# Attention with a noisy top-2 router on one core: another order around the last attention tile, and one-hots of two groups on ScalarE

## The chip, the cores and the metric

The kernel runs on one core of a Trainium2 chip. A core has five engines with an instruction queue each: TensorE (PE: matmuls and transposes; its weight loads are listed apart as PEld), VectorE (DVE), ScalarE (ACT), GpSimd (POOL) and SyncE (SP, which here only issues DMAs). Each works through its queue in order and waits on semaphores for the others; transfers are done by 16 DMA engines that all queues share. The metric is the device time of one execution in microseconds; the time before is the median of three runs.

## The reference

Chunked attention with a few memory rows, then a mixture of experts in which each row goes to its two best experts. Cut to what matters:

```python
# attention: B 4, H 8, S 768, D 64; chunks of 32 rows, context 16 left, 8 right, 8 memory rows
scores = scale * q_c @ concat(mem_k, k_ctx).T
a = exp(scores - scores.max(-1));  a = a / (a.sum(-1) + 1e-9)
out = a @ concat(mem_v, v_ctx)
# router: x (3072, 512), 8 experts
noisy = x @ w_gate + log1p(exp(x @ w_noise)) * noise
top2 = the two largest of noisy per row;  top2_w = softmax over these two
# experts
for e in range(8): out[rows with e] += top2_w * (relu(x[rows] @ w1[e]) @ w2[e])
```

## The kernel before

**Attention.** The 3072 rows are cut into 12 tiles of 256 rows. A loop of slots (-1 to 11) runs a software pipeline: slot i makes the scores of tile i+1 and the values of tile i, and turns the x rows of tile i-1 (in the last slot also those of tile 11) for the router's gate. The order inside a slot is written out by hand, as one string of letters per slot (ORDERS), and the queues of TensorE, ScalarE, VectorE and SP follow that order. GpSimd has its own queue: pinned instructions keep the order in which the program calls them, and its work on the routing is put among them as it is called.

The letters that matter here: S scores, s their maximum and subtraction (settle_s, L530 and L532), E the exponential (L603), W the transposes of a window of values (p_v, L490), w and y their copy to SBUF. The copy of the second window also issues, on SP, two DMAs that bring the memory rows of values next to it (mvn, L500) and two that store finished x rows to DRAM (xd, L679). P is the transpose of the probabilities (p_p, L610), p its copy (pT, L616), V the row sums and values (ps_g L623, ps_o L630; ps_o reads the window and the memory rows), i the reciprocal, v and v1 the two norms (L643), X, X2 and X3 transposes of x rows, x, x2 and x3 their copies to xT, G the gate (ps_l, L665), g and r its copy to lg on VectorE or ScalarE.

**Routing.** A Route handles a group of tiles: R[0] tiles 0 to 6, R[1] tiles 7 to 9, R[2] tiles 10 and 11. Since a tile has two halves of 128 rows, they have 14, 6 and 4 half tiles. N starts a route and makes its noise on ScalarE (two ACTIVATEs, L293 and L294). C steps through `choose` on VectorE, 14 instructions that find the two best experts and code the pair (the matrix M, in ohp). K ranks the rows of each pair on TensorE (`ranks`, p_rank) and adds up the counts on GpSimd (`total`, cum; the next group's ranks need it). H turns p_rank into one rank per row. O (`slots`) makes a one-hot of 96 places per row, `weights` and `values` the numbers that are to be listed (row, row of the output, three parts of a weight, a flag), on GpSimd for R[0] and R[1]. Q and q multiply one-hots with the first two values on TensorE: the list of rows (`list_rows`, L384). F does the same with the other four (`list_facts`, L389). Letter a adds the lists of rows and makes main_src, the indices of the first gather. Rows past the 96 places of a pair go to a rest list: I (`rest_onehots`) makes one-hots of 64 rest places, T (`rest_list`, L403) multiplies them.

**Experts.** After slot 11 the rows are gathered by index from xd (L978, GpSimd), 96 for each pair of experts; the first eight tiles are turned on TensorE (p_xt, L1204), later ones by transposing DMAs. Then the eight experts follow one another (p_h L1032, p_y L1096), with weights in five rotating places. `load_layer(2, 0)` is the first load of expert 2, 1 MB, issued on GpSimd behind slot 9:

```python
    WHEN = {9: [(2, 0)]}
```

It stands in GpSimd's queue ahead of the weights of R[1].

Of the kernel before, what the change touches and what calls it, by code (L numbers as in the profile page):

```python
# [16 lines left out]
Alu = mybir.AluOpType  # L17
# [6 lines left out]
def kernel(  # L24
# [14 lines left out]
    nc = tc.nc  # L39
# [237 lines left out]
    class Route:  # L277
# [64 lines left out]
        def weights(self, eng):  # L342
            d = self.tile([128, self.n], F32, "d")
            eng.tensor_tensor(out=d, in0=self.mm[:, 1], in1=self.mm[:, 0], op=Alu.subtract)
            for i in range(3):
                eng.tensor_copy(self.f[:, :, 2 + i], d)
                if i < 2:
                    eng.tensor_tensor(out=d, in0=d, in1=self.f[:, :, 2 + i], op=Alu.subtract)
            self.eng.tensor_tensor(out=self.f[:, :, 5], in0=self.ii[:, 0], in1=self.ii[:, 1], op=Alu.is_gt)
# [17 lines left out]
        def slots(self):  # L367
            n, eng = self.n, self.eng
            self.oh_l = (self.tile([128, n, MT], BF16, "oh_l") if self.last else
                         nat[2 * self.k].rearrange("p g c -> p (g c)")[:, 0:n * MT].rearrange("p (n t) -> p n t", n=n))  # L370
            eng.tensor_tensor(out=self.oh_l, in0=bc(self.rr, MT), in1=io_l[:, 0:MT].unsqueeze(1).to_broadcast([128, n, MT]), op=Alu.is_equal)
# [20 lines left out]
    def rest_onehots(r):  # L392
        t1 = const.tile([128, r.n], F32, name=f"t1{r.k}")
        nc.vector.tensor_scalar(out=t1, in0=r.rr, scalar1=float(MT), scalar2=None, op0=Alu.is_ge)
        k2 = const.tile([128, r.n], F32, name=f"k2{r.k}")
        nc.vector.scalar_tensor_tensor(out=k2, in0=r.rr, scalar=1.0 - MT, in1=t1, op0=Alu.add, op1=Alu.mult)
        nc.vector.tensor_tensor(out=oh_t[:, r.g0:r.g0 + r.n], in0=bc(k2, RU),
                                in1=io_1[:, 0:RU].unsqueeze(1).to_broadcast([128, r.n, RU]), op=Alu.is_equal)
# [293 lines left out]
    def decode(L, n, name, src=None, pool=const):  # L692
# [27 lines left out]
    WHEN = {9: [(2, 0)]}  # L720
# [14 lines left out]
    ]  # L735

    with tc.manual_schedule(engines={ET.PE, ET.Activation, ET.DVE, ET.SP}):
# [11 lines left out]
        def close(r):  # L749
            advance(r.chain)  # L750
            if r.last:
                r.values(nc.gpsimd, 0, 2)
            else:
                r.weights(nc.gpsimd)
                r.values(nc.gpsimd, 0, NV)

        def weigh(r):
            r.weights(nc.vector)
            r.values(nc.vector, 2, NV)
# [10 lines left out]
        def slot(i):  # L770
# [124 lines left out]
            for g, x in enumerate("AB"):  # L895
# [5 lines left out]
                      Q=lambda r: (r.list_rows(p1[:, 0], r is R[-2], r is R[-1]), r.list_facts(p2, r is R[-2], r is R[-1])),  # L901
                      q=lambda r: r.list_rows(p1[:, 0], r is R[-2], r is R[-1]),
                      F=lambda r: r.list_facts(p2, r is R[-2], r is R[-1]))
            for k in ORDERS[i + 1].split():
# [6 lines left out]
                elif k == "Y":  # L911
                    pin(nc.gpsimd.indirect_dma_start(out=turning[3].bitcast(F32)[0:MT, 0:E], out_offset=None, in_=moe_w_gate,
                                                     in_offset=bass.IndirectOffsetOnAxis(ap=ready[0:MT], axis=0)))
                elif k[0] == "I":
                    rest_onehots(R[int(k[1])])
# [5 lines left out]
                elif k == "a":  # L921
                    nc.vector.tensor_tensor(out=src[0:MT], in0=p1[:, 0], in1=listed[0:MT, 0], op=Alu.add)
                elif k[0] in rs and k not in fs:
                    rs[k[0]](R[len(RG) - 1 if k.endswith("2") else -1 if i < NT - 1 else len(RG) - 2])
                else:
                    fs[k]()
# [5 lines left out]
            for e, n in WHEN.get(i, ()):  # L932
                load_layer(e, n)
# [624 lines left out]
```

## Time and profile before

| | |
|---|---|
| Median of three runs | 334.56 us (334.29, 334.56, 336.42) |
| Profiled execution, its own time | 333.11 us |
| Its span, first to last instruction | 331.5 us |
| Mean granted TensorE clock | 0.926 |
| TensorE busy | 278.4 us (84%) |
| VectorE, ScalarE, GpSimd busy | 185.7 (56%), 153.5 (46%), 209.0 us (63%) |
| TensorE busy from 105 to 130 us | 3.25, 2.95, 3.87, 3.38, 4.51 of every 5 us |
| TensorE busy from 130 to 150 us | 10.00 and 9.95 of every 10 us |

How to read it: a busy share is an average over the program. Up to about 104 us the attention keeps four engines busy side by side; from about 135 us on TensorE does the experts with hardly a pause. Between these lies the routing of the last tiles, where every engine waits for another. Rows of a timeline give the start, the length, the engine, the line, what is written and read, how many instructions were merged, and in brackets how long the engine had stood idle before and what released it.

### The profile page before, as it was taken

What the parts mean: (1) busy time and instruction counts of PE and PEld (TensorE: products, weight loads), DVE (VectorE), ACT (ScalarE), POOL (GpSimd) and SP (SyncE); (2) the same over time, 40 slices, a digit from 0 to 9 for tenths busy, and PEclk for the clock granted to TensorE, in tenths of its full rate; (3) what the DMA queues carried; (4) which work ended last, traced back from release to release, by engine and by line L of the source; (5) the groups of instructions that cost most, each with busy time, mean ns of one, the idle gap of its engine ahead of it and who ended that gap; (6) DMA issues with size and microseconds to landing.
All of it is one profiled execution on the core that took longest, in us unless ns stands there. A gap on an engine that the chain in (4) does not pass through costs nothing.

```text
span 331.5 us, 9214 instructions
## 1 busy us (share of the span) xinstructions
PE 278.4 (84%) x3746; PEld 206.3 (62%) x3762; DVE 185.7 (56%) x418; ACT 153.5 (46%) x316; POOL 209.0 (63%) x304
## 2 busy tenths in 40 slices
PE   0566979888799578999999999999999999999920
PEld 0455867777677368866766775585676666767400
DVE  4765755979798885644653443835345345443520
ACT  5666644766676202535453453453543534525210
POOL 4679595999482457767768675743754744735370
PEclk9969797999979755999999999999999999999975
DMA  7999959988926513435587895998979789522141
GB/s 126 212 211 192 216 109 219 219 138 119 225 51 117 132 30 80 97 79 111 86 182 123 87 182 120 191 217 143 224 151 215 171 158 186 130 83 74 58 145 37
DMA packets 43501, 46.79 MB, mean 141 GB/s; under 512 B 20465, under 2 KB 33845, under 8 KB 43452
## 3 DMA queue, kind: packets, MB, share of 16 engines
q0 software_dynamic: 23024, 38.27, 60.3%
q1 hardware_dynamic: 19884, 7.83, 11.7%
q8 instruction: 31, 0.51, 0.6%
q14 instruction: 18, 0.15, 0.1%
q10 hardware_dynamic: 544, 0.03, 0.1%
HBM read 59.11 MB, written 11.33 MB: 212 GB/s over the span
## 4 chain that ended last, share of the span: by engine, by line
PE 59%; DMA 6%; DVE 6%; issue 3%; ACT 2%; POOL 1%; POOLq 0%; SPq 0%; DVEq 0%; ACTq 0%
PE p_h L1032 28%; PE p_y L1096 21%; DMA w_all<-mvn 5%; PE p_y L1151 2%; PE p_v L490 1%; POOL out_dram L983 1%; PE ps_o L630 1%; ACT pT L616 1%; PE p_t L461 1%; DMA xt<-xd,main_src 1%; ACT w_all L465 1%; PE p_xt L1204 1%; PE p_p L610 0%; PE p_x L652 0%; PE p_rank L338 0%
## 5 line engine op out<-in xcount | busy, mean ns | idle before, releaser
L1032 PE MATMUL p_h<-w_all 128*128 128x288 bf16 (+3 forms) x1120 | 97.5, 248 | 0.7 <-ACT w_all L465 0.5
L1032 PEld LDWEIGHTS <-w_all 128*128 128x128 bf16 x1120 | 83.6, 99 | 14.0 <-issue 2.1
L1096 PE MATMUL p_y<-w_all 128*128 128x512 bf16 x368 | 83.6, 379 | 2.1 <-DVE yq L1090 0.8
L1020 ACT ACTIVATE w_all<-p_h 128x288 bf16<-128x288 f32 (+3 forms) x137 | 46.8, 375 | 45.4 <-PE p_h L1032 42.3
L1096 PEld LDWEIGHTS <-w_all 128*128 128x128 bf16 x384 | 37.1, 98 | 43.6 <-issue 2.1
L437 POOL COPY w_all<-w_all 128x512 bf16<-128x512 bf16 (+1 forms) x59 | 42.9, 795 | 12.2 <-PE p_t L461 7.4
L1018 DVE TENSOR_SCALAR w_all<-p_h 128x288 bf16<-128x288 f32 (+1 forms) x65 | 30.7, 476 | 34.2 <-PE p_h L1032 34.0
L983 POOL DMA_INDIRECT out_dram<-y,main_dst x24 | 22.8, 949 | 18.6 <-DMA w_all<-in_moe_w_dram 5.8
L1105 DVE SCALAR_TENSOR_TENSOR y<-p_y,main_w,y 96x512 f32<-96x512 f32 x24 | 17.9, 747 | 26.0 <-PE p_y L1096 26.0
L978 POOL DMA_INDIRECT xt<-xd,main_src x28 | 26.0, 928 | 10.0 <-issue 7.0
L1090 ACT COPY yr<-p_y 32x512 f32<-32x512 f32 x24 | 13.9, 579 | 36.4 <-DVE y L1105 34.6
L1101 ACT ACTIVATE y<-p_y,main_w 96x512 f32<-96x512 f32 x24 | 16.4, 683 | 21.5 <-PE p_y L1096 21.5
L461 PE MATMUL p_t<-identf,w_all 128*128 128x128 f32 x120 | 19.0, 297 | 1.8 <-ACT pT L616 0.8
L1000 POOL DMA_INDIRECT out_dram<-yB,rd x8 | 9.3, 1160 | 16.8 <-DVE yB L1157 15.6
L1090 DVE COPY yr<-p_y 32x512 f32<-32x512 f32 x12 | 8.3, 694 | 19.8 <-ACT y L1101 19.8
L1262 POOL DMA_INDIRECT fr<-tdr,adr x16 | 16.0, 1000 | 4.9 <-issue 4.6
L978 POOL DMA_INDIRECT xt<-xd,rs x16 | 14.8, 925 | 6.7 <-issue 3.4
L490 PE MATMUL p_v<-identf,w_all 128*128 128x128 f32 x96 | 16.4, 312 | 2.8 <-ACT w_all L465 1.8
L643 DVE TENSOR_TENSOR w_all<-ps_o,rs 128x512 bf16<-128x512 f32 x24 | 15.7, 683 | 5.0 <-PE ps_o L630 4.2
L461 PEld LDWEIGHTS p_t<-identf,w_all 128*128 128x128 f32 x120 | 14.3, 152 | 3.5 <-issue 1.6
L465 ACT COPY w_all<-p_v 128x512 f32<-128x512 f32 x21 | 12.0, 587 | 9.1 <-PE p_v L490 9.0
L1090 DVE COPY yq<-p_y 32x512 f32<-32x512 f32 x12 | 8.3, 694 | 12.9 <-ACT y L1101 12.8
(237 smaller groups left out, 419.6 us busy)
## 6 DMA issues: line engine op xcount, KB each, us to landing
w_all<-in_moe_w_dram POOLq DMA_DIRECT2D x12, 1024.0 KB
w_all<-in_moe_w_dram POOLq DMA_DIRECT2D x16, 256.0 KB
w_all<-in_k_dram POOLq DMA_DIRECT2D x4, 768.0 KB
w_all<-in_q_dram POOLq DMA_DIRECT2D x4, 768.0 KB
w_all<-in_v_dram POOLq DMA_DIRECT2D x4, 768.0 KB
xd<-w_all SPq DMA_DIRECT2D x24, 128.0 KB
w_all<-mvn SPq DMA_DIRECT2D x24, 32.0 KB
w_all<-xt SPq DMA_TRANSPOSE x39
```

The lines of the kernel that those rows point to most:

```text
L437: i = eng.tensor_copy(to, x)
L461: nc.tensor.transpose(out=p_t[:, s, :], in_=m.bitcast(F32)[:, s * 128:(s + 1) * 128], identity=identf)
L490: nc.tensor.transpose(out=p_v[:, i, c, :], in_=vT[:, c, c0:c0 + 128], identity=identf)
L978: pin(nc.gpsimd.indirect_dma_start(out=t[0:n].bitcast(I32), out_offset=None, in_=src_, in_offset=bass.IndirectOffsetOnAxis(ap=ix, axis=0)))
L983: i = nc.gpsimd.indirect_dma_start(out=out if rows is None else rows, out_offset=bass.IndirectOffsetOnAxis(ap=ix, axis=0), in_=y, in_offse ...
L1018: nc.vector.tensor_scalar(out=out_, in0=in_, scalar1=0.0, scalar2=None, op0=Alu.max)
L1020: nc.scalar.activation(out=out_, in_=in_, func=Act.Relu)
L1032: nc.tensor.matmul(out=o if len(xk.shape) == 2 else o.rearrange("p (j t) -> p j t", j=xk.shape[1]), lhsT=w_all[:, e % WR, kp * F + f * 128 ...
L1090: (nc.scalar.copy if eng else nc.vector.tensor_copy)(to, p[MT:128, :])
L1096: nc.tensor.matmul(out=p, lhsT=h[:, f, k, :], rhs=w2(e, f), start=(f == 0), stop=(f == FB - 1))
L1101: nc.scalar.activation(out=y[0:MT], in_=p[0:MT], func=Act.Copy, scale=wt)
L1105: nc.vector.scalar_tensor_tensor(out=y[0:MT], in0=p[0:MT], scalar=wt, in1=y[0:MT], op0=Alu.mult, op1=Alu.add)
```

## The change

Everything in it concerns slots 9 to 11 and the routing of the three groups.

- Slot 9 and 10: the one-hots of R[0] (O) go from slot 9 to slot 10, behind the reciprocal; the list of R[0] (L) goes from the front of slot 10 to its end. Both windows of values are transposed and copied ahead of the transposes of tile 10's probabilities, and the maximum and subtraction of tile 11 (s) stand ahead of tile 10's values.
- The load of expert 2 is called at the end of slot 10 (LL), no longer at the end of slot 9.
- Slot 11: both norms of tile 11 (v, v1) stand ahead of the second half of R[1]'s choice. The list of R[1] is split: its rows (Q1) come ahead of R[2]'s ranks, its facts (F1) and all of the rest list (T00, T01, T1, T2) come behind the last list of rows (q2).
- One-hots of R[1]'s places and of the rest places of R[0] and R[1] are made on ScalarE by `ones_at`: the square of the difference per half tile, then relu(1 - square) over all. The two steps before them (`rest_places`) stay on VectorE; R[2]'s stay there altogether.
- R[1]'s weights are called by themselves (d1), its values in two parts on GpSimd: 0 and 1 when its choice is closed, 2 to 5 when R[2]'s is.

```diff
-            self.eng.tensor_tensor(out=self.f[:, :, 5], in0=self.ii[:, 0], in1=self.ii[:, 1], op=Alu.is_gt)
+
+        def flags(self):
+            nc.vector.tensor_tensor(out=self.f[:, :, 5], in0=self.ii[:, 0], in1=self.ii[:, 1], op=Alu.is_gt)
...
-            eng.tensor_tensor(out=self.oh_l, in0=bc(self.rr, MT), in1=io_l[:, 0:MT].unsqueeze(1).to_broadcast([128, n, MT]), op=Alu.is_equal)
+            if self.k == 1:
+                ones_at(self.oh_l, io_l[:, 0:MT], self.rr)
+            else:
+                nc.vector.tensor_tensor(out=self.oh_l, in0=bc(self.rr, MT),
+                                        in1=io_l[:, 0:MT].unsqueeze(1).to_broadcast([128, n, MT]), op=Alu.is_equal)
...
+    def ones_at(to, at, x, lo=0, hi=None, last=True):
+        for g in range(lo, to.shape[1] if hi is None else hi):
+            nc.scalar.activation(out=to[:, g], in_=at, func=Act.Square, scale=-1.0, bias=x[:, g:g + 1])
+        if last:
+            nc.scalar.activation(out=to, in_=to, func=Act.Relu, scale=-1.0, bias=1.0)
+
+    def rest_places(r):
...
+        r.k2, r.squares = k2, 0
+
+    def rest_onehots(r, n=None):
+        oh = oh_t[:, r.g0:r.g0 + r.n]
+        if r.last:
+            nc.vector.tensor_tensor(out=oh, in0=bc(r.k2, RU), in1=io_1[:, 0:RU].unsqueeze(1).to_broadcast([128, r.n, RU]), op=Alu.is_equal)
+        else:
+            lo, r.squares = r.squares, r.n if n is None else r.squares + n
+            ones_at(oh, io_1[:, 0:RU], r.k2, lo, r.squares, last=n is None)
...
-    WHEN = {9: [(2, 0)]}
...
-        "S M W P X y s W p y L x l V i v E G v1 r",
-        "P N p X C1 C1 V i I0 x v G X2 C1 C1 D1 K1 x2 v1 X3 x3 p2 g H1 G2 r2 O1 Y N2 p1 C2 C2 C2 Q1 T00 C2 D2 K2 T01 H2 O2 I1 q2 T1 a B2 F2 I2 T2",
+        "S M W y W s P y X p x V i O v E v1 G L l r LL",
+        "N P p C1 X V i x v v1 G J0 I0.3 X2 C1 d1 r x2 X3 c1 x3 c1 G2 r2 N2 K1 D1 p2 p1 I0.8 C2 H1 O1 Y C2 C2 D2 Q1 K2 H2 O2 q2 a F1 I0 T00 T01 J1 I1 T1 B2 F2 J2 I2 T2",
...
             if r.last:
                 r.values(nc.gpsimd, 0, 2)
+                R[1].values(nc.gpsimd, 2, NV)
+            elif r.k:
+                r.flags()
+                r.values(nc.gpsimd, 0, 2)
             else:
                 r.weights(nc.gpsimd)
+                r.flags()
                 r.values(nc.gpsimd, 0, NV)
...
-                      Q=lambda r: (r.list_rows(p1[:, 0], r is R[-2], r is R[-1]), r.list_facts(p2, r is R[-2], r is R[-1])),
+                      Q=lambda r: r.list_rows(p1[:, 0], r is R[-2], r is R[-1]),
...
+                elif k == "d1":
+                    R[1].weights(nc.gpsimd)
+                elif k == "LL":
+                    load_layer(2, 0)
...
-            for e, n in WHEN.get(i, ()):
-                load_layer(e, n)
```

How the queues stand before and after, at the places that matter. A row has the line, the operation, and what is written from what. Lines after the change are those of the changed file.

GpSimd, around the load of expert 2, before (cum is the sum of R[0], d the weights of R[1]):

```order
L364 TENSOR_TENSOR red<-red 128x28 x6
L365 TENSOR_TENSOR cum_2414<-cum_141,red 128x28
L83 DMA w_all<-in_moe_w_dram 128x4x1024
L344 TENSOR_TENSOR d<-mm 128x6
L346 CAST facts<-d 128x6
```

The same place after:

```order
L366 TENSOR_TENSOR red<-red 128x28 x6
L367 TENSOR_TENSOR cum_2414<-cum_141,red 128x28
L83 DMA w_all<-in_moe_w_dram 128x4x1024
L344 TENSOR_TENSOR d<-mm 128x6
L346 CAST facts<-d 128x6
```

Nothing moved here. GpSimd further on, in slot 11, before (values of R[1] in one piece, its cum, the small gather of Y, the first values of R[2]):

```order
L362 TENSOR_TENSOR red<-ohp 128x84
L378 TENSOR_TENSOR w_all<-ohp,facts 128x1008
L364 TENSOR_TENSOR red<-red 128x28 x2
L365 TENSOR_TENSOR cum_2819<-cum_2414,red 128x28
L912 DMA w_all<-in_moe_w_gate_dram,ready 96x8
L378 TENSOR_TENSOR vals_last<-ohp,facts 128x4x56
```

After:

```order
L364 TENSOR_TENSOR red<-ohp 128x84
L384 TENSOR_TENSOR w_all<-ohp,facts 128x6x56
L366 TENSOR_TENSOR red<-red 128x28
L936 DMA w_all<-in_moe_w_gate_dram,ready 96x8
L366 TENSOR_TENSOR red<-red 128x28
L384 TENSOR_TENSOR w_all<-ohp,facts 128x6x112
L367 TENSOR_TENSOR cum_2844<-cum_2414,red 128x28
L384 TENSOR_TENSOR vals_last<-ohp,facts 128x4x56
```

The sum cum of R[1] stands behind the small gather and behind the second part of the values. ScalarE in slot 11, before, from the xT copy of tile 10 to the first copy for the experts:

```order
L465 COPY xT<-p_x 128x512
L465 COPY xT<-p_x 128x256 x2
L465 COPY lg<-ps_l 128x32
L293 ACTIVATE ns_last<-lg 128x32
L294 ACTIVATE ns_last<-ns_last 128x32
L465 COPY w_all<-p_xt 128x384
```

After (k_2788 are the rest places of R[0], rank those of R[1]'s list):

```order
L484 COPY xT<-p_x 128x512
L400 ACTIVATE w_all<-io_130,k_2788 128x64 x3
L484 COPY lg<-ps_l 128x32
L484 COPY xT<-p_x 128x256 x2
L484 COPY lg<-ps_l 128x32
L293 ACTIVATE ns_last<-lg 128x32
L294 ACTIVATE ns_last<-ns_last 128x32
L400 ACTIVATE w_all<-io_130,k_2788 128x64 x8
L400 ACTIVATE w_all<-io_l,rank 128x96 x6
L402 ACTIVATE w_all<-w_all 128x576
L400 ACTIVATE w_all<-io_130,k_2788 128x64 x3
L402 ACTIVATE w_all<-w_all 128x896
```

Three squares now precede the copies that the gate of tile 11 needs, and eight precede the one-hots of R[1]. TensorE at the last ranks (p_rank of R[2]), before, with a matmul of the rest list ahead:

```order
L403 LDWEIGHTS w_all
L403 MATMUL ps_o<-w_all 64x168
L334 LDWEIGHTS tri
L334 MATMUL p_rank<-ohp,tri 128x112
L335 LDWEIGHTS ones
L335 MATMUL p_rank<-cum_2819,ones 128x112
```

After:

```order
L390 LDWEIGHTS w_all
L390 MATMUL p_list<-w_all 96x28
L334 LDWEIGHTS tri
L334 MATMUL p_rank<-ohp,tri 128x112
L335 LDWEIGHTS ones
L335 MATMUL p_rank<-cum_2844,ones 128x112
```

In both the list rows of R[1] (p_list, 96x28) stand ahead of the last ranks; its facts and the first ten matmuls of the rest list stood between them before, and now only the list rows do.

More of the change, by code (lines that the diff above doesn't have):

```diff
@@ L913, in slot @@
                                                      in_offset=bass.IndirectOffsetOnAxis(ap=ready[0:MT], axis=0)))
+                elif k[0] == "J" and k != "J":
+                    rest_places(R[int(k[1])])
                 elif k[0] == "I":
[L915 removed]
+                    rest_onehots(R[int(k[1])], int(k[3:]) if len(k) > 2 else None)
+                elif k == "d1":
+                    R[1].weights(nc.gpsimd)
+                elif k == "LL":
+                    load_layer(2, 0)
                 elif k[0] == "T":
```

8 lines of the change are left out of this document (3 added, 5 removed), and 2 rows, old and new, of the table ORDERS.

## The prediction

> **What bounds the kernel now.** I read the page first (span, clock row), then the chain of waits, then the stretch from 99 to 136 us engine by engine, since every edit lies there, and last the busy time and granted clock in stretches cut where the clock changes. The profiled execution took 333.11 us for its span; the runs of before have a median of 334.56 us, 1.45 us more. The sum below is made on the profile's axis, and its difference is added to the median.
>
> ```profile
> span 331.5 us, 9214 instructions
> ```
>
> The chain of waits, start and length in us, from the end of the attention part into the first expert:
>
> ```profile
> 104.19 7.30 DMA w_all<-mvn
> ...
> 111.53 0.72 PE ps_o L630 x59
> ...
> 112.28 0.69 DVE w_all L643
> ...
> 116.80 1.14 PE p_list L384 x12
> 117.94 0.62 PE p_list L389 x6
> 118.56 1.54 PE ps_o L403 x10
> 120.10 0.26 PE p_rank L334
> ...
> 123.67 2.62 DMA xt<-xd,main_src
> ...
> 126.34 0.50 PE p_xt L1204 x4
> ...
> 135.57 4.72 PE p_h L1032 x48
> ```
>
> The reader is to see four things. The values of the last tile (L630) end a wait for a transfer at 111.53. From there a chain of small steps, mostly on VectorE, runs to the row indices (main_src), and the first gather is issued at 123.67. Its rows are turned on TensorE at 126.34. From 135.57 TensorE works almost without a pause to the end, so what the change moves at 135.57 it moves at the end.
>
> Busy time in stretches that follow the clock (the seventh column is the granted clock):
>
> ```profile
> 91.18:94.60 3.42, 3.06 (x22) 2.67 (x22) 3.08 (x11) 1.95 (x4) 1.97 (x7) 0.50 0.14 23
> ...
> 104.84:108.25 3.41, 3.14 (x106) 2.36 (x104) 2.70 (x8) 2.77 (x6) 0.00 (x0) 1.00 1.07 200
> 108.25:111.66 3.41, 0.59 (x41) 0.48 (x42) 2.94 (x11) 0.44 (x1) 1.61 (x5) 1.00 1.03 272
> 111.66:115.07 3.41, 2.70 (x82) 2.23 (x71) 2.58 (x9) 0.37 (x1) 1.47 (x4) 0.50 0.03 11
> ...
> 125.31:128.73 3.42, 2.93 (x40) 2.56 (x41) 0.96 (x5) 0.48 (x1) 2.51 (x4) 0.50 0.39 103
> 128.73:132.14 3.41, 3.41 (x37) 3.27 (x36) 2.64 (x14) 1.46 (x3) 2.60 (x3) 0.50 0.34 91
> ```
>
> After a stretch with TensorE busy 0.59 of 3.41 us the clock is at half from 111.66. It comes back at 132.14, after a stretch busy throughout; 2.93 of 3.42 did not bring it back, 3.06 of 3.42 (at 91.18) did.
>
> **The load moved: 0.** The order of GpSimd shows the 1 MB load in the same place as before, between the sum of the first group (cum) and the weights of the second: its queue holds nothing for slot 10, so a line at the end of slot 10 issues when one at the end of slot 9 did.
>
> ```profile
> 100.98 0.80 POOL L83 DMA_DIRECT2D w_all<-in_moe_w_dram  x1
> 101.21 1.37 SPq L679 DMA_DIRECT2D xd<-w_all  x2
> ...
> 103.39 1.48 SPq L500 DMA_DIRECT2D w_all<-mvn  x2
> ```
> ```profile
> 102.25:110.75 8.50, 5.61 (x147) 4.52 (x146) 7.26 (x22) 4.81 (x9) 0.78 (x4) 1.00 1.00 194
> ```
>
> SP's order is unchanged too: the rows of memory (mvn) stand behind two stores of xd, and from 102.25 to 110.75 the DMA engines are busy 1.00 at 194 GB/s. So the 111.53 stays.
>
> **The last tile's softmax ahead: 0.** The second window is settled before pT, so mvn can be issued some 0.8 us earlier (102.6 for 103.39), and the softmax of tile 11 begins when the 1.56 us one-hots no longer stand ahead of it. But TensorE now has the list of the first group ahead of tile 11, and the values still wait for mvn. Both gains end in the wait to 111.53; that wait is their cover. What is given up: VectorE used it for half of the second group's choice and for the rest one-hots (the 1.12 us row below). Now both norms stand ahead of that half, so VectorE idles there.
>
> **VectorE behind 111.53.**
>
> ```profile
> 110.01 0.11 DVE L394 TENSOR_SCALAR t<-rank 128x14 f32<-128x14 f32 x1
> ...
> 110.36 1.12 DVE L397 TENSOR_TENSOR w_all<-k,io 128x896 bf16<-128x896 f32 x1
> ...
> 112.89 0.20 DVE L303 TENSOR_TENSOR c<-c,desc 128x48 f32<-128x48 f32 x1
> ...
> 113.81 0.17 DVE L349 TENSOR_TENSOR facts<-ii 128x6 bf16<-128x6 f32 x1
> ...
> 114.77 0.33 DVE L353 TENSOR_TENSOR ohr<-ohp,p_rank 128x168 f32<-128x168 bf16 x1
> ...
> 115.49 1.25 DVE L371 TENSOR_TENSOR w_all<-rank,io_l 128x576 bf16<-128x576 f32 x1
> 116.88 0.19 DVE L311 TENSOR_TENSOR nl_last<-ns_last,nz 128x32 f32<-128x32 f32 x1
> ...
> 119.75 0.27 DVE L328 TENSOR_TENSOR ohp<-pcode,pc_last 128x112 bf16<-128x112 f32 x1
> ```
>
> New order: two norms from 112.28 (2 x 0.69, to 113.6), the two small steps for the rest places (0.35, from 110.01 to 110.36), then ten steps of the second group. Five of them took 1.09 (112.89 to 113.98), so ten take 2.2, to 116.15; that is 2.2 us later than the 113.98 of before. The 1.25 us one-hots are gone from VectorE. What then starts the last group's choice is its noise on ScalarE.
>
> **One-hots on ScalarE.** In place of one instruction per group stand one ACTIVATE per half tile, with a pointer as bias, and one Relu.
>
> ```profile
> 102.77 0.59 ACT L465 COPY w_all<-p_v 128x512 f32<-128x512 f32 x1
> 103.25 0.60 ACT L465 COPY xT<-p_x 128x512 f32<-128x512 f32 x1
> ...
> 115.40 0.37 ACT L465 COPY xT<-p_x 128x256 f32<-128x256 f32 x1 [1.28 <-PE p_x L652]
> ...
> 116.61 0.23 ACT L294 ACTIVATE ns_last<-ns_last 128x32 f32<-128x32 f32 x1
> ```
> ```profile
> L1101 ACT ACTIVATE y<-p_y,main_w 96x512 f32<-96x512 f32 x24 | 16.4, 683 | 21.5 <-PE p_y L1096 21.5
> L1090 ACT COPY yr<-p_y 32x512 f32<-32x512 f32 x24 | 13.9, 579 | 36.4 <-DVE y L1105 34.6 <-issue 1.8
> ...
> L170 ACT CAST wgn<-w_all 128x64 bf16<-128x64 f32 x1 | 0.2, 239 | 0.0
> ```
>
> A square of 128x64 is not in the trace. The cast of that shape takes 0.24; a pointer operand adds 0.10 (0.683 against 0.579); a next one starts 0.11 before the end of the last (103.25 against 103.36). Bounds: 0.15 each (overlap, no pointer) and 0.34 (pointer, no overlap); I take 0.25, with both, and 0.275 for 128x96. The Relu of 128x576 I take as 0.66, a little over the 0.60 of 128x512. The Trainium skill (ScalarE: Activation LUTs, "What ACT_TABLE_LOAD costs") gives 280 ns + 0.833 ns per element with a pointer bias and an overlap of 93 ns, an estimate of 0.24 and 0.27; by it the sum would be the same within 0.1 us, and by its rules for kernel authors, which give such work to VectorE, this edit is the wrong way round. No run here shows that yet; the rows say the same of size: 6 x 0.275 + 0.66 = 2.3 us for 1.25.
>
> Three squares from 113.95 end at 114.8. The lg copy (under 0.23) and the first xT copy put the second xT copy at 115.2; before it was at 115.40, and noise was ready 1.44 later (116.84). So noise is ready at 116.6. VectorE: 14 steps took 116.88 to 120.02, 3.14, and ranking the second group 0.72 (114.77 to 115.49), now between them: that rank stands at 116.6 + 1.1 + 0.7 = 118.45 and the last choice at 120.5 (before 120.02). ScalarE has eight squares ahead, to 118.7; six squares of the second group to 120.35; Relu to 121.0. TensorE's order puts that group's list rows (1.14) ahead of the last ranks: 122.2, and the ranks end 0.5 later at 122.7. Before they ended at 120.61. So main_src and the first gather are **2.1 us later, at 125.8**. Ends of the ScalarE price: 1.4 and 3.5 us.
>
> **GpSimd: covered, by 0.85 us.**
>
> ```profile
> L378 POOL TENSOR_TENSOR w_all<-ohp,facts 128x1008 bf16<-128x1008 bf16 x1 | 1.9, 1877 | 0.0
> L912 POOL DMA_INDIRECT w_all<-in_moe_w_gate_dram,ready x1 | 1.1, 1064 | 0.6 <-issue 0.6
> ```
>
> The sum cum, which the last ranks read, now stands behind the small gather (0.6 + 1.06) and four of six parts of the values (two thirds of 1.88). From the second maximum (114.9) I count to 121.5; it is wanted at 122.35. If 0.85 us is lost there, cum is late next.
>
> **Rest places behind the list.** 10 matmuls of facts (0.10 each, L389) and 24 of the rest list (0.154 each, L403) now follow the last list rows without a gap: 4.7 us at half clock, with drains 4.9, from 124.8 to 129.6. Before they filled pauses. So TensorE is late next: the first turn of gathered rows at 129.6 for 126.34. But that makes TensorE busy throughout 125.31 to 128.73, and by the rows above the clock comes back at 128.73, not 132.14; the turn is then at 129.2. From 126.34 to 135.57 TensorE did 5.8 us at half clock and 3.43 at full, 6.33 us of full clock: 129.2 + 6.33 = 135.5. The gathers are slower:
>
> ```profile
> 131.03 0.91 POOL L978 DMA_INDIRECT xt<-xd,main_src  x1 [0.30 <-issue]
> ...
> 145.86 0.91 POOL L978 DMA_INDIRECT xt<-xd,rs  x1 [1.38 <-DVE rs L1280]
> ```
>
> The seventh, issued at 131.03 and landed 2.62 later, comes 2.1 later, at 135.75; with its turn the long stretch begins near 136.0 for 135.57: **+0.45 us**. Behind it GpSimd's own lateness is taken up by its 1.38 us of idle time at 145.86.
>
> The Trainium skill (TensorE: Matmul & The Clock Gate, "What's actually happening") says the 3.4 us window runs free and does not start with the kernel. By it the return would lie anywhere between 127.3 and 130.7, and the sum between +0.4 and +0.9; this one trace shows one phase only.
>
> **The rivals.**
> - Memory rows earlier. If mvn lands with its issue, 0.8 us earlier, or the load does stand back and the wait is gone (pT allows 109.95, 1.6 earlier), the gather is late by 1.3 or 0.5 us, and the stretch starts 0.2 to 0.7 earlier: 333.9 to 334.4. For it: the rows above, by which the load's bytes are most of what mvn queues with. Against: the unchanged order of GpSimd and SP, and DMA engines at 1.00.
> - The clock comes back at 132.14 as before. By then 1.27 us of the 6.33 are done, the rest ends at 137.2: +1.6, 336.2. For it: 2.93 of 3.42 was not enough.
> - Slower by over 1%. One mechanism: the pause between the turn and the first p_h, or a wait in the rest list, breaks two stretches, and the half clock lasts to 138.97. Then 4.7 of 6.33 us are done there, and the stretch begins at 140.6: +5.0, 339.6. It decides from a return at 135.6 on, where the loss is 3.3.
> - That the change does little is the forecast itself: the load does not move and the softmax is hidden.
>
> **How the numbers follow.** 1% is 3.35 us, about what a measurement of this kernel can tell from no change. Forecast (+0.45, 335.0): 0.52. Memory rows earlier: 0.17. Clock as before: 0.19. Half clock on: 0.07. For a gain over 1% I find no mechanism, and keep 0.05 for one unseen. So faster 0.05, slower 0.07, same 0.88. The range runs from the low ScalarE price together with the earlier rows (333.2) to the high price (gather +3.5, stretch +1.9) with a late clock (337.0).
>
> **What would show it.** The load issued near 101 and ps_o released near 111.5: the load did not move. One square every 0.25 us. The last ranks starting right behind the second group's list rows near 122.2. First gather near 125.8, no pause on TensorE from 125 to 129, clock 1.00 from about 128.7, the long stretch from about 136. The sum is wrong if ps_o starts before 110.5, if the first gather is issued before 124.5, or if the clock is still at half at 131.

## The result, and the profile after

| | before | changed |
|---|---|---|
| Median of the runs | 334.54 us (9 runs, 333.06 to 339.91) | 337.49 us (9 runs, 335.05 to 340.08) |
| Profiled execution, span | 333.11, 331.5 us | 339.69, 338.1 us |

The ratio is 1.0102 (95% interval 1.0066 to 1.0137); a second set of runs gave 1.0135 (1.0093 to 1.0178). It compares the fast runs of each kernel alone, so it is not the ratio of the two medians. The forecast was 335.0 with a range to 337.0: the loss was seen too small.

The chain of waits of the changed kernel, from the memory rows to the first turn (start, length, what):

```profile
108.98 7.53 DMA w_all<-mvn
...
116.55 0.76 PE ps_o L649 x60
...
117.33 1.29 DVE w_all L662 x2
...
121.79 0.68 DVE nl_last L313
...
123.78 1.71 ACT w_all L400 x6
125.51 0.69 ACT w_all L402
...
126.24 1.14 PE p_list L390 x12
...
128.97 0.82 PE p_list L390 x8
129.79 0.62 PE p_list L395 x6
130.41 3.11 PE ps_o L422 x20
...
134.76 0.43 PE p_xt L1232 x4
```

The squares and the Relu (L400, L402) stand in it, and the list of rest places (L422) between the rows of the list and the first turn. But ps_o is 5.0 us later than before (116.55 for 111.53), and that can't all be the change: the choice of the first group starts in code that both kernels share, and it is 5.9 us late already. Timelines of two profiles of each kernel, before (first two rows) and changed:

```profile
89.44 0.21 DVE L311 TENSOR_TENSOR nl<-ns,nz 128x112 f32<-128x112 f32 x1
```
```profile
95.14 0.21 DVE L311 TENSOR_TENSOR nl<-ns,nz 128x112 f32<-128x112 f32 x1
```
```profile
95.31 0.21 DVE L311 TENSOR_TENSOR nl<-ns,nz 128x112 f32<-128x112 f32 x1
```
```profile
89.56 0.21 DVE L311 TENSOR_TENSOR nl<-ns,nz 128x112 f32<-128x112 f32 x1
```

Each kernel has an early and a late run. So I measure from this start, called c0. All numbers are differences of starts in the timelines, in us; ps_o is the start of its main group of matmuls (63 or 64 of them). The last but one column is c0 to the first turn, the last c0 to the first p_y; it is empty for runs on other chips (see below).

| kernel | load issued | ps_o | ps_o to first gather | ps_o to first turn | c0 to turn | c0 to p_y |
|---|---|---|---|---|---|---|
| before | +11.54 | +22.09 | 12.14 | 14.81 | 36.90 | 50.90 |
| before, again (e2) | +12.84 | +19.75 | 12.46 | 15.12 | 34.87 | 48.47 |
| changed | +11.55 | +21.24 | 14.24 | 18.14 | 39.38 | 51.43 |
| changed, again (e1) | +11.56 | +21.23 | 14.23 | 18.10 | 39.33 | 51.65 |
| e3 first rest one-hots on VectorE | +11.55 | +21.66 | 13.93 | 17.89 | 39.55 | 51.74 |
| e4 second one-hots on VectorE | +11.56 | +21.19 | 15.05 | 18.83 | 40.02 | 52.17 |
| e8, e13 slot 10 alone | +11.5 | +21.27, +20.81 | 12.10, 12.39 | 14.86, 15.04 | 36.13, 35.85 | |
| e17 before, load first | +10.59 | +21.58 | 12.39 | 15.04 | 36.62 | |
| e18 changed, one-hots back | +12.95 | +20.09 | 14.55 | 18.45 | 38.54 | |
| e9, e14 before, load late | +26.1 | +18.38, +18.38 | 13.82, 13.91 | 16.55, 16.58 | 34.93, 34.96 | |
| e5, e11 load late, turn ahead of list | +26.3 | +18.22, +18.76 | 14.68, 14.29 | 18.13, 18.16 | 36.35, 36.92 | |
| e10, e15 all of it | +22.5 | +18.65, +18.59 | 13.47, 13.20 | 16.23, 16.31 | 34.88, 34.90 | |

Behind ps_o the change costs 1.4 to 1.7 us at the first p_y (30.19 and 30.42 for 28.81 and 28.72). Ahead of it, it gains 0.9 against the first profile of before and loses 1.5 against the second.

Two more readings of these traces say how far c0 and this table carry. From the first p_y to the end of the span it takes 191.1 to 191.4 us in five of the six profiles whose runs took 333 to 340 us (before, e2, changed, e3, e4) and 192.5 in e1, so that c0 and the last column make up most of what differs between these runs. And c0 does not follow the change: in all 20 traces of this document it lies between 89.4 and 95.7, with a mean of 92.6 in the five traces of the kernel before with its slots 9 and 10 as they were (before, e2, e9, e14, e17) and of 92.6 in the 15 others.

### The profile page after: what moved, and what is told of

Its sections match the earlier page's. It is cut to its first block, busy times and chain, and to the rows that moved or that the text cites. A ratio compares the mean times of both kernels' runs of the same rounds, so it can differ in the third digit from the quotient of the medians.

```text
span 338.1 us, 9255 instructions
## 1 busy us (share of the span) xinstructions
PE 279.9 (83%) x3762; PEld 206.5 (61%) x3762; DVE 184.4 (55%) x414; ACT 162.3 (48%) x346; POOL 208.0 (62%) x305
## 4 chain that ended last, share of the span: by engine, by line
PE 45%; DMA 6%; DVE 5%; issue 4%; POOL 3%; ACT 1%; POOLq 1%; DVEq 0%; ACTq 0%
PE p_h L1060 22%; PE p_y L1124 18%; DMA out_dram<-y,main_dst 4%; POOL out_dram L1011 2%; DMA w_all<-mvn 2%; PE p_y L1179 2%; PE ps_o L422 1%; ACT w_all L400 1%; PE p_list L390 1%; DVE yq L1118 0%; DVE w_all L662 0%; POOLq L1581 0%; PE p_list L395 0%; PE p_xt L1232 0%; DVE w_all L484 0%
## 5 line engine op out<-in xcount | busy, mean ns | idle before, releaser
L1060 PE MATMUL p_h<-w_all 128*128 128x288 bf16 (+3 forms) x1120 | 95.7, 245 | 1.0 <-ACT w_all L484 0.7
L1060 PEld LDWEIGHTS <-w_all 128*128 128x128 bf16 x1120 | 82.0, 98 | 14.4 <-issue 2.4
L1124 PE MATMUL p_y<-w_all 128*128 128x512 bf16 x384 | 85.8, 379 | 1.2 <-DVE yq L1118 0.8
L1124 PEld LDWEIGHTS <-w_all 128*128 128x128 bf16 x384 | 37.1, 98 | 43.5 <-issue 2.0
L456 POOL COPY w_all<-w_all 128x512 bf16<-128x512 bf16 (+1 forms) x59 | 42.9, 786 | 11.5 <-PE p_t L480 7.0
L480 PE MATMUL p_t<-identf,w_all 128*128 128x128 f32 x120 | 19.9, 306 | 1.4 <-ACT pT L635 0.8
L509 PE MATMUL p_v<-identf,w_all 128*128 128x128 f32 x96 | 15.5, 301 | 2.8 <-ACT w_all L484 1.8
L480 PEld LDWEIGHTS p_t<-identf,w_all 128*128 128x128 f32 x120 | 15.1, 157 | 3.1 <-issue 1.7
L635 ACT COPY pT<-p_p 128x1024 bf16<-128x1024 bf16 x11 | 11.2, 1014 | 11.3 <-PE p_p L629 10.8
```

The source lines that it names most:

```text
L456: i = eng.tensor_copy(to, x)
L480: nc.tensor.transpose(out=p_t[:, s, :], in_=m.bitcast(F32)[:, s * 128:(s + 1) * 128], identity=identf)
L1060: nc.tensor.matmul(out=o if len(xk.shape) == 2 else o.rearrange("p (j t) -> p j t", j=xk.shape[1]), lhsT=w_all[:, e % WR, kp * F + f * 128 ...
L1124: nc.tensor.matmul(out=p, lhsT=h[:, f, k, :], rhs=w2(e, f), start=(f == 0), stop=(f == FB - 1))
```

## The experiments

The runs from e5 on are from other chips, which ran the kernel before in 417 to 423 us. There TensorE stands still in the experts without a wait that the profile shows ("issue"); of e5, what was waited for between 128 and 230 us (total, times, longest), where the trace of before shows no such row among its first:

```profile
PE p_h L1060 <- issue: 18.9, 15, 3.5
```

So of those kernels the traces are read up to the first turn only, and their ratios stand for those chips. In e6, e7, e12 and e16 VectorE's work on the ranks of the first group came at +10.6 to +12.5 (elsewhere +9.7 to +10.3), after stretches at a clock of 0.50 to 0.87, and ps_o at +23 to +26; these four are used behind ps_o only.

**Both kernels again (e1, e2), no edit.**

> The changed kernel once more, for a second profile. In the first one the last tile's ps_o was released 5.0 us later than before (116.55 against 111.53), after a stretch whose code is the same in both kernels, and the long stretch of the feed-forward came 6.45 us later (141.86 against 135.41). Theory A (the stretch up to tile 10 varies from run to run and the change costs only what lies behind ps_o, 1.4 us): ps_o is released within 1 us of 111.5 here, or the kernel before shows such a delay too; the time is near 335.5 to 336. Theory B (the change brings the delay ahead of ps_o): ps_o again 3 us or more late, the time 337 to 339. Both: 14.2 us from the release of ps_o to the first gather, against 12.1.

> The kernel before once more, for a second profile. Ratio 1.00. Theory A: the release of ps_o moves by more than 1 us between the two profiles of the same kernel. Theory B: it stays within 0.5 us of 111.5 unless the run is one of the longer ones. Both: 12.1 us from there to the first gather.

Measured: e1 1.0135 (above), e2 1.0021 (0.9984 to 1.0057). The stretch ahead of c0 varies in both kernels, as theory A has it; but the changed kernel is slower in the second set too, and ps_o varies behind c0 only in the kernel before.

**One-hots back on VectorE (e3, e4).** Diff of e3, its strings cut to the letters that change, and of e4:

```diff
-        if r.last:
+        if r.last or r.k == 0:
...
-v1 G L l r LL
+v1 G L J0 I0 l r LL
-G J0 I0.3 X2
+G X2
-p1 I0.8 C2
+p1 C2
-F1 I0 T00
+F1 T00
```
```diff
-            if self.k == 1:
+            if self.k == 3:
```

> The first group's rest one-hots on VectorE again, in its pause of 2.2 us ahead of the second group's choice; all else as in the changed kernel. If the eleven squares that stand between other work of ScalarE delay the last tile's transposed copies (0.82 us) or the second group's squares, the first gather comes 0.2 to 0.8 us earlier, 13.4 to 14.0 us behind ps_o. If they lie in pauses (the squares of the second group waited 0.35 us for their ranks), it stays at 14.2 and the time is that of the changed kernel within 0.3 us. If VectorE's 1.12 us are not hidden, it is later by up to 1.1.

> The second group's one-hots on VectorE again, at the same place of the order. Theory S (six squares and the Relu, 2.4 us on ScalarE, hold up the second group's list rows and so the last ranks): the list rows start 1.2 to 1.7 us earlier and the first gather with them, 12.5 to 13.0 us behind ps_o, ratio to before 1.4 us lower. Theory V (the last group's choice on VectorE ends just as late, because two of its steps stand for 0.5 and 1.4 us beside GpSimd's multiplications): the one-hots now push that choice back by 0.7 to 1.25 us, and the first gather is 0 to 1.0 us later, 14.2 to 15.2 us behind ps_o.

Measured: e3 1.0054 (1.0021 to 1.0086), first gather 0.3 us earlier; e4 1.0133 (1.0086 to 1.0180), first gather 0.8 us later: theory V. In e4 the one-hots take 2.26 us, with GpSimd's multiplication beside them until 123.24 (alone they take 0.76, see e7 below):

```profile
121.61 2.26 DVE L376 TENSOR_TENSOR w_all<-rank,io_l 128x576 bf16<-128x576 f32 x1
...
121.91 1.33 POOL L384 TENSOR_TENSOR w_all<-ohp,facts 128x672 bf16<-128x672 bf16 x1
```

e3 is 0.8% better than e1 on the same chip, some 2.7 us, while its trace shows 0.3 at the gather and nothing at the first p_y. Where that difference arises is not shown. The 20 values of c0 scatter with a standard deviation of 2.2 us, so by an estimate from them chance can make a good part of it between 12 runs and 6.

**The held step (e6), and all edits behind ps_o (e7, e16).** In e6 the multiplication over 128x672 is recorded behind the last sum; e7 has this, both one-hots on VectorE, and T00 T01 in a pause (e16 is e7 once more):

```diff
-                R[1].values(nc.gpsimd, 2, NV)
...
-Q1 K2 H2 O2 q2
+Q1 K2 H2 O2 vv q2
...
-D2 Q1 K2
+D2 T00 T01 Q1 K2
```

> The changed kernel with GpSimd's multiplication over 128x672 behind the last sum. Port theory (a VectorE step with two operands in SBUF stands while GpSimd's multiplication runs): the step ns_last takes 0.19 to 0.2 us for 1.59, and the last group's choice ends 1.4 us earlier, 8.9 us behind ps_o for 10.26. The first gather then gains little, 0 to 0.3 us, since the second group's list rows, which wait for the squares and their Relu, still stand ahead of the last ranks on TensorE. Rival (some other cause, a semaphore or the small gather): ns_last stays over 1 us.

> The changed kernel with both one-hots on VectorE (the first group's in its pause), GpSimd's multiplication over 128x672 behind the last sum, and 14 of the rest-list matmuls in TensorE's pause ahead of the second group's list rows. If the squares and the held choice together make the first gather late, it comes 12.9 to 13.5 us behind ps_o for 14.24, and TensorE's part between gather and first turn falls from 3.9 to about 2.7; the long stretch's first p_y stands 28.5 to 29.2 us behind ps_o for 30.2 to 30.4. Ratio to the changed kernel 0.995 to 0.997. If the cause is elsewhere (the order of the norms and choices), the gather stays at 14 or more.

> The changed kernel with the one-hots on VectorE, the held multiplication moved and 14 rest-list matmuls in a pause, but with the load and the list where the change has them. First gather 12.85 us behind ps_o (changed kernel 14.24), first turn 17.0 (18.1). So 1.1 to 1.4 us under the changed kernel: ratio to before 1.006 to 1.010. If it is at 1.002 or less, more of the loss lies in those one-hots than the trace up to the first turn shows.

The timeline of the changed kernel, and that of e6:

```profile
123.87 1.59 DVE L319 TENSOR_TENSOR ns_last<-desc,ii_last 128x32 f32<-128x32 f32 x1
...
124.07 1.33 POOL L384 TENSOR_TENSOR w_all<-ohp,facts 128x672 bf16<-128x672 bf16 x1
```
```profile
123.69 0.19 DVE L319 TENSOR_TENSOR ns_last<-desc,ii_last 128x32 f32<-128x32 f32 x1
```

The step falls from 1.59 to 0.19 and the last choice ends 1.4 us earlier (8.88 behind ps_o for 10.26), yet the first gather stays (14.25): the list rows behind the squares stood ahead of the last ranks. So two chains end together ahead of the gather, and freeing one shows nothing. With both freed (e7, e16) it comes at 12.85 and 13.07, the first turn at 17.03 and 17.25. In e7 the one-hots then take 0.76 us:

```profile
120.91 0.76 DVE L378 TENSOR_TENSOR w_all<-rank,io_l 128x576 bf16<-128x576 f32 x1
```

Ratios: e6 1.0110 (1.0040 to 1.0181), e7 0.9955 (0.9904 to 1.0006), e16 1.0019 (0.9979 to 1.0059). e16 expected 1.006 to 1.010 and named 1.002 or less as the sign that more of the loss lies in these edits than the trace shows up to the first turn. That sign came, as in e3: the run times put more of the loss behind ps_o than the traces do.

**Slot 10 alone (e8, e12, e13).** The kernel before with the strings of slots 9 and 10 of the change (three traces of one kernel):

```diff
-        "W S P W y p M s X V i x E v v1 K H O G y r",
-        "S M W P X y s W p y L x l V i v E G v1 r",
+        "W S P W y p M s X V i x E v v1 K H G y r",
+        "S M W y W s P y X p x V i O v E v1 G L l r",
```

> The kernel before with only the two strings for tiles 9 and 10 of the change: the last tile's softmax ahead, the first group's one-hots later, nothing of the squares and of the rest places. If the whole loss lies behind ps_o, the time is that of before (ratio 0.998 to 1.002) and the first gather stands 12.1 to 12.5 us behind ps_o. If the new order holds up ps_o itself (TensorE's list matmuls and the turn of probabilities at half clock), ps_o stands at +21.2 also where the run is late, where the kernel before had +19.8, and the ratio is 1.002 to 1.006.

> The two strings for tiles 9 and 10 alone once more, on a chip whose times can be compared. The first trace had ps_o at +21.27 with the choice starting late (95.3), where the kernel before had +19.75 at the same start, and the first gather 12.10 us behind ps_o as before. So the ratio should be 1.001 to 1.005, a part of the changed kernel's 1.010 to 1.0135; if it is 0.998 to 1.000, the whole loss lies in the order behind ps_o.

> The two strings for tiles 9 and 10 alone, third trace; wanted is a time on a chip that runs the kernel before in 334 us. First gather 12.1 us behind ps_o as before. If the order ahead of ps_o carries a part of the loss (ps_o at +21.2 from the start of the first group's choice in early and late runs, where the kernel before had +22.1 in an early run and +19.8 in a late one), the ratio is 1.000 to 1.005; the rest to 1.010 and 1.0135 lies behind ps_o. If the order ahead of ps_o carries nothing, 0.998 to 1.001.

Ratios 0.9954 (0.9891 to 1.0018), 0.9963 (0.9912 to 1.0013), 0.9963 (0.9915 to 1.0011). The traces agree with the second reading (+21.27 and +20.81 in runs that start at 95.3 and 93.7), the times with neither: all three ratios lie below 1, so on those chips the 1 to 1.5 us ahead of ps_o do not show. In e12 the first gather came 13.3 us behind ps_o, where 12.1 was expected.

**The load against the memory rows (e17, e18).** In e17 GpSimd issues the load between two sums; e18 is the changed kernel with O where it was:

```diff
-    WHEN = {9: [(2, 0)]}
+    WHEN = {}
...
+                if self.k == 0 and g == 4:
+                    pin(r_)
+                    load_layer(2, 0)
```
```diff
-K H G y r
+K H O G y r
...
-V i O v E
+V i v E
```

> The kernel before with one edit: the 1 MB load between the fourth and the fifth partial sum of the first group on GpSimd's queue, so that it is always issued ahead of the tile-11 memory rows, near +10.7 from the start of the first group's choice. In the second trace of the kernel before, VectorE's one-hots (1.56 us) held GpSimd's sums (3.14 us for 1.84), the load went out at +12.84, level with the rows, and ps_o was released at +19.8; in the first trace they did not meet, the load went out at +11.54, and ps_o at +22.1. Theory H (the load's place against the rows decides, and the changed kernel always has the load first, because it moved those one-hots): ps_o at +21 to +22.5 with a wait for the rows of 1 us or more, and a time 1 to 2.3 us over before, ratio 1.003 to 1.007. Rival (the late start of the run made the difference): ps_o near +19.8 where the choice starts near 95, near +22 where it starts near 89, and no change of time.

> The changed kernel with one edit: the first group's one-hots on VectorE back in tile 9's string, right behind the ranks. Theory H: they hold GpSimd's sums again (six sums 3.1 us for 1.85), the load goes out at +12.8 behind or level with the rows, and the rows land 1.3 to 2.3 us earlier; ps_o then waits for TensorE's chain (list, turn, copy) instead, and since the exponentials come 1.6 us later it gains 0 to 1 us against +21.2. Rival: the load stays at +11.5 and ps_o waits for the rows as in the changed kernel. Behind ps_o all as in the changed kernel (first gather at 14.2).

First the kernel before in the profile of the prediction: the six sums take 1.84 us, and the one-hots (L371) start when the last sum (cum) is already running.

```profile
98.83 1.84 POOL L364 TENSOR_TENSOR red<-red 128x28 f32<-128x28 f32 x6
...
100.75 0.24 POOL L365 TENSOR_TENSOR cum<-cum,red 128x28 bf16<-128x28 bf16 x1
100.91 1.56 DVE L371 TENSOR_TENSOR w_all<-rank,io_l 128x1344 bf16<-128x1344 f32 x1
...
111.53 0.70 PE L630 MATMUL ps_o<-w_all,pT 64*32 64x64 bf16 x63 [1.12 <-DMA w_all<-mvn]
```

Then the timeline of e2, the kernel before in its other form: the one-hots (L371) start while GpSimd adds up, its six sums take 3.14 us where the first profile had 1.84, and the load goes out level with the rows (mvn).

```profile
104.54 3.14 POOL L364 TENSOR_TENSOR red<-red 128x28 f32<-128x28 f32 x6
...
106.02 1.56 DVE L371 TENSOR_TENSOR w_all<-rank,io_l 128x1344 bf16<-128x1344 f32 x1
...
107.98 0.80 POOL L83 DMA_DIRECT2D w_all<-in_moe_w_dram  x1
107.99 1.48 SPq L500 DMA_DIRECT2D w_all<-mvn  x2
...
114.89 0.73 PE L630 MATMUL ps_o<-w_all,pT 64*32 64x64 bf16 x63 [1.17 <-DMA w_all<-mvn]
```

The changed kernel: the one-hots come behind the load, so nothing holds the sums.

```profile
104.71 1.85 POOL L366 TENSOR_TENSOR red<-red 128x28 f32<-128x28 f32 x6
...
106.86 0.80 POOL L83 DMA_DIRECT2D w_all<-in_moe_w_dram  x1
...
108.18 1.48 SPq L519 DMA_DIRECT2D w_all<-mvn  x2
109.03 1.49 DVE L376 TENSOR_TENSOR w_all<-rank,io_l 128x1344 bf16<-128x1344 f32 x1
```

e17, where the load is forced ahead of the rows in a run that starts as late as e2 (c0 at 95.68):

```profile
106.27 0.80 POOL L83 DMA_DIRECT2D w_all<-in_moe_w_dram  x1
...
108.52 1.48 SPq L503 DMA_DIRECT2D w_all<-mvn  x2
...
117.26 0.94 PE L633 MATMUL ps_o<-w_all,pT 64*32 64x64 bf16 x64 [3.14 <-DMA w_all<-mvn]
```

e18, where the one-hots hold the last sum (cum, 1.66 us where it took 0.24) and with it the load:

```profile
105.61 1.66 POOL L367 TENSOR_TENSOR cum<-cum,red 128x28 bf16<-128x28 bf16 x1
105.61 1.56 DVE L376 TENSOR_TENSOR w_all<-rank,io_l 128x1344 bf16<-128x1344 f32 x1
...
107.22 0.80 POOL L83 DMA_DIRECT2D w_all<-in_moe_w_dram  x1
...
107.86 1.48 SPq L519 DMA_DIRECT2D w_all<-mvn  x2
...
114.36 0.68 PE L649 MATMUL ps_o<-w_all,pT 64*32 64x64 bf16 x64
```

Theory H stands in the traces: with the load first, the rows take 8.7 us from issue to ps_o in e17 and ps_o waits 3.14 for them, in a late run, as they took 8.1 in the profile above, an early one. With the load held (e18), ps_o is 1.1 us earlier than in the changed kernel and waits for no transfer. In the changed kernel the rows are not the only thing that ends there: the row sums (ps_g), which need the turned probabilities, start at +19.6 in e1, and ps_o waits 1.1 us for the rows behind them; in the other profile of the changed kernel, with the clock at 0.50 from 111.66 to 115.08, they start at +20.6, and 0.15 of that wait is left. The price in time is not shown: e17 1.0022 (0.9978 to 1.0066), and e18 has no ratio.

**The load really late (e9, e14; e5, e11; e10, e15).** In e9 it stands behind the second group's values and sum. e5 is the changed kernel with the load behind the small gather and P ahead of the list; e10, and e15 once more, has the edits of e7 on top, but with the load behind the first step of the weights, and it also moves steps of the second group's choice, the adding of the first group's list (l0, to a place behind O2) and the rest one-hots of the second group. The diffs of e9 (first) and e5, cut to the letters that change:

```diff
-C1 C1 D1 K1 x2
+C1 C1 D1 K1 LL x2
```
```diff
-v1 G L l r LL
-N P p C1
-O1 Y C2
+v1 G r
+N P L0 p l0 C1
+O1 Y LL C2
```

> The kernel before with one edit: the 1 MB load behind the second group's values and sum on GpSimd's queue, some 16 us later than it was, so that it really moves. If the memory rows' landing sets the release of ps_o, that wait (1.12 us at +22.1 behind the start of the first group's choice, or at +19.8 in a late run) goes, ps_o is released 1.0 to 1.6 us earlier, and the time falls by as much, ratio 0.995 to 0.998. The rival: the load now lies beside the first gathers (12.1 us behind ps_o) and holds them up by up to 1 us; then the ratio is 0.998 to 1.002. If the load had nothing to do with that wait, ps_o stays.

> The kernel before with the load really late. In its first trace ps_o was released at +18.4 without a wait for the memory rows, but the first norm waited 1.1 us for VectorE, and the first turn came at +34.9 (before: 36.9 with an early start of the choice, 34.9 with a late one). So a gain of 0 to 2 us: ratio 0.994 to 1.000.

> The changed kernel with the 1 MB load really later (behind the small gather on GpSimd's queue) and with the turn of the last tile's probabilities ahead of the first group's 42 list matmuls. Measured from the start of the first group's choice, ps_o was released at +21.2 in the changed kernel, at +22.1 and +19.8 before. If the memory rows (mvn) that queue with the load set that point, they land 2 us or more earlier and ps_o goes at +18 to +19, and the time falls by 2 to 3 us against the changed kernel (ratio to before about 1.003). If TensorE's list at half clock sets it, the same follows from the other edit, and the trace shows which of the two ps_o still waits for. If neither, ps_o stays at +21 and the time too. GpSimd's order behind it shifts as well: the multiplication over 128x672 stands behind the last group's values here, so the long step of the last choice (1.59 us) should be gone or moved.

> The kernel with the load late and the turn of probabilities ahead of the list once more: the chip of its first run spent 84 us more in every kernel behind the first gather, so that its time says little. ps_o again at +18 to +19, no wait for the memory rows; the first gather 14.2 to 14.7 us behind it; ratio to before 1.001 to 1.005, that is 2.5 to 3 us under the changed kernel. If the ratio stays at 1.010 or more, the 3 us gained ahead of ps_o are lost behind it.

> The changed kernel with the load behind the first step of the second group's weights, the turn of probabilities ahead of the first group's list, all one-hots that precede the first gather on VectorE, the multiplication over 128x672 behind the last sum, and 14 rest-list matmuls in TensorE's pause. From the start of the first group's choice: ps_o at +18 to +19 (changed kernel +21.2), first gather 12.8 to 13.5 us behind it (14.24), first turn at +34 to +35 in all (39.3; before 36.9 and 34.9). If these are the causes, the time is 3 to 4 us under the changed kernel and 0 to 1.5 us under before: ratio 0.995 to 1.000.

> The changed kernel with the load late, the turn of probabilities ahead of the list, the one-hots on VectorE and the held multiplication moved: first turn at +34.9 in its first trace, 39.3 in the changed kernel. If what the traces show up to the first turn carries the whole loss, the time is 3.5 to 4.5 us under the changed kernel, ratio to before 0.996 to 1.001.

In all six ps_o comes at +18.2 to +18.8 and waits for no transfer. e9 and e14 show by one edit that the memory rows were the bound in the kernel before; in the other four the turn of probabilities moves with the load, and the runs do not separate the two. In e9 VectorE takes the gain back against e2 (first turn at +34.93 for +34.87; +36.90 in the first profile). The timeline has the row of values done at 109.33, and the first norm 1.8 us behind it, after the rest one-hots:

```profile
108.65 0.68 PE L632 MATMUL ps_o<-w_all,pT 64*32 64x64 bf16 x64
...
110.13 1.12 DVE L399 TENSOR_TENSOR w_all<-k,io 128x896 bf16<-128x896 f32 x1
...
111.17 0.68 DVE L645 TENSOR_TENSOR w_all<-ps_o,rs 128x512 bf16<-128x512 f32 x1
```

Ratios: e9 0.9975 (0.9938 to 1.0011), e14 0.9964 (0.9918 to 1.0010), e5 0.9971 (0.9917 to 1.0025), e11 0.9961 (0.9922 to 1.0001), e10 1.0037 (1.0002 to 1.0071), e15 1.0002 (0.9954 to 1.0051). None is shown to beat the kernel before. On these chips the times do not follow the first turn either: e10, with +34.88, has a higher ratio than e11, with +36.92.

## Why the prediction was wrong

- **The load moved: 0.** This step failed. The order of GpSimd's queue is unchanged, as it said, but I took the place in a queue for the time of issue. In the kernel before the load's issue hangs on VectorE's one-hots of 1.56 us: where they meet GpSimd's sums, they hold them by 1.3 us. The change moves those one-hots, and the load is always ahead of the rows. The profile on which the sum was made is the other case, in which they missed each other (one-hots at 100.91, last sum running from 100.75): against it the load did not move (+11.55 for +11.54), against e2 it goes out 1.3 us earlier. Of five traces with these one-hots in their old place in the kernel before or its variants (before, e2, e9, e14, e17) four show sums held. Against its own profile the forecast sum held (c0 to p_y +0.5 and +0.75 for +0.45), but by luck: ps_o came 0.85 earlier where it had 0, and 1.4 and 1.6 were lost behind ps_o. Against the other it is +3.0 and +3.2, inside the first measured interval (2.2 to 4.6 us) and at the lower edge of the second (3.1 to 5.9): 1.5 of it lies ahead of ps_o, of which e18 takes 1.1 back, and the rest behind. How many of the timed runs of before had the held form is not recorded, and slot 10 alone (e8, e12, e13) showed no loss in time. So the traces show the mechanism; that it makes the measured loss is an estimate from them.
- **So the 111.53 stays.** Against the first profile ps_o was 0.85 earlier from c0: the rows were issued 1.1 us earlier behind the load, and landed with that, which is the rival "memory rows earlier". It was outweighed by what lies behind.
- **First gather +2.1.** Right, and through the chain that it named: 14.24 and 14.23 for 12.14 (12.46 in e2). Squares of 128x64 took 0.25, those of 128x96 0.28 (six in 1.71 in the chain above), the Relu 0.69. In the timeline of the changed kernel:

```profile
121.42 2.00 ACT L400 ACTIVATE w_all<-io,k 128x64 bf16<-128x64 bf16 x8
```

  The Trainium skill's estimates from a pointer bias (ScalarE: Activation LUTs, "What ACT_TABLE_LOAD costs"), 0.24 and 0.27, agree within 0.02.
- **VectorE.** The noise came where it was put (5.0 behind ps_o for 5.07), the last choice did not: two of its steps stood for 0.48 and 1.40 us beside GpSimd, which the step had not seen. By itself it cost nothing (e6), but it turned the one-hots back on VectorE into a loss (e4). The 1.25 us that the prediction set against ScalarE's 2.3 for these one-hots was such a hold too: in the profile before they stood beside GpSimd's multiplication (114.25 to 116.13), and alone they took 0.76 (e7).
- **GpSimd: covered.** The sum cum was ready 9.0 us behind ps_o and the ranks that read it came at 10.7. What GpSimd cost was not its own lateness, but VectorE's.
- **Rest places +0.45.** The term was mis-sized: 1.43 at the long stretch (25.31 behind ps_o for 23.88). The first turn came 18.14 behind ps_o for the 17.67 of the forecast, and from there to the long stretch (141.86) went 7.2 us for 6.8. One wait there was not in the sum: in e1 the long stretch stands 0.31 us for ScalarE's last step on main_w, at the end of a row of small steps on the lists. The clock, of the changed kernel by stretches:

```profile
125.31:128.73 3.42, 1.47 (x17) 1.35 (x17) 2.44 (x11) 2.51 (x6) 1.69 (x6) 0.50 0.00 0
128.73:132.14 3.41, 3.17 (x27) 3.05 (x28) 2.26 (x13) 1.78 (x7) 1.33 (x3) 0.50 0.00 0
132.14:135.55 3.41, 3.41 (x36) 2.48 (x35) 1.38 (x6) 0.60 (x2) 2.66 (x3) 0.57 0.31 87
```

A mean of 0.57 means that it came back at 135.1 (2.93 of 3.41 us at half), 18.5 behind ps_o where the forecast had 17.2. In e1 it came back at about 128.8, 18.0 behind:

```profile
128.73:132.14 3.41, 2.98 (x64) 2.65 (x63) 1.73 (x10) 1.74 (x4) 2.75 (x3) 0.99 0.38 108
```

Half clock lasted to about the first turn and not beyond.
- **The rivals.** The clock "as before" came nearest to what is lost behind ps_o (+1.6), but by its number only: it had the return 20.6 behind ps_o, and it came 18.5 and 18.0 behind. The lasting half clock did not happen. The forecast had no rival in which the load goes out earlier.

Open: what moves c0 between 89.4 and 95.7 us, in code that no kernel here touches; 2.4 us of e3; the run times of e7, e16 and of slot 10 alone, which put the loss behind ps_o; and the price of the load's place in run time on a chip of 334 us.

## What to carry to other kernels

A place in a queue is not a time: before costing a moved instruction at nothing, ask what delayed the ones ahead of it, and whether that moves. Two profiles of the kernel before would have shown that its bound had two forms; a sum made on one profile holds for its form. Where two chains end together, undoing one need not show anything, so undo both.

## What the runs showed of the hardware

VectorE and GpSimd held each other for whole instructions: 0.19 us became 1.59 beside a GpSimd multiplication of 1.33, six sums of 1.84 became 3.14 beside one-hots of 1.56, and one sum of 0.24 became 1.66. The Trainium skill (SBUF — State Buffer, "SBUF: two separate sides") has the port pair of the two as an exclusive lock, held for a whole instruction by whichever starts first, and among those concerned are VectorE's instructions with two inputs in SBUF, against a GpSimd instruction that reads SBUF. The traces agree on the hold, and the held steps of the last choice are of that kind. Who had the lock first can't be read from the starts alone: the step of 1.59 us is recorded from 123.87, ahead of the multiplication at 124.07. That such a hold decides where a load stands against a DMA of another queue, 8.1 to 8.7 us from issue to use behind it (before, changed, e17) and 6.9 level with it (e2), I had not expected.
